# Batch 1's last three stores between batch 3's loads, one of them as five transfers, and batch 2's gather and MLP sooner

## The chip, the cores and the metric

The kernel runs on one core of one Trainium2 chip. The metric is the device time of one execution in microseconds, as a median over runs. The kernel before has a median of 256.77 us over 3 runs (256.72 to 257.05).

## The reference

Two stages over `q`, `k`, `v` of 4 batches x 6208 rows x 256 columns, all in f32:

```python
qn = q / (norm(q, axis=1) + 1e-06);  kn = k / (norm(k, axis=1) + 1e-06)   # over the rows
a = softmax(kn.transpose(0, 2, 1) @ qn / tau)       # 256 x 256 per batch
x = v @ a
scores[b] = x[b] @ w_gate                           # one number per row
top_idx = the 128 rows of the batch with the largest score
ye = relu(x[b, top_idx] @ w1) @ w2                  # w1 256x1024, w2 1024x256
out[b] = x[b];  out[b, top_idx] += sigmoid(scores[b, top_idx])[:, None] * ye
```

So every batch reads q, k and v once (6.36 MB each), writes its output once, and rewrites 128 rows of it.

## The kernel before

The rows of a batch are cut into chunks of 1024 rows, each as 128 partitions x 8 rows x 256 columns, and one remainder of 64 rows; `lorder` takes them as 0, remainder, 1, 2, 3, 4, 5. A load of a chunk reads 1 MB of f32 and writes 512 KB of bf16; all loads are issued by GpSimd (POOL) on its own queue (`emit_load`, L256). `pump` (L292) issues the next load when its buffer is free and the loads in flight are worth less than `AHEAD` = 12 us. Stores of a chunk are 128 partitions of 8 KB, 1 MB, issued by SyncE (SP) in `emit_store` (L721), called from `out_store` (L1098); batch 3's chunks go as two half stores.

A batch goes through these steps. TensorE multiplies q and k as they come (L448 and L452; for batch 3 L463, with norms apart); ScalarE and VectorE make the softmax from the sums (`softmax_stages`, L468). v is transposed on TensorE (`p2_transpose`, L572, matmul L583) and copied out of PSUM (L611, L614). The scores are products of the transposed v with `a @ w_gate` (L641, L651). `select_stages` (L737) then finds the 128 best rows: seven rounds of a comparison (L791), a counting matmul (L811) and a reduction (L815), then the index (L873), a gather of these 128 rows of v by POOL (L879), their transposes (L904), x of these rows (L919), the MLP (L945, ReLU L951, L967) and the update `upd` (L981), which POOL scatters into the output (L994) once the batch's stores have landed. Beside this, `p2_out` (L667) makes the output groups of 4 rows per partition: matmul L689, copy to a staging tile L707 or L704. There are 9 staging tiles.

What differs between the batches. All stores of batches 2 and 3 and those of batch 1's last two chunks are held until a gate, the landing of the first half of the last v load (`GATE`, L238, and the loop at L1142); one of batch 1's two is issued by POOL behind the last load. Batch 2's MLP is split: after its gather and first transposes the generator yields `("dead", f)` (L935 and L936), and goes on only when TensorE has ended batch 3's q/k products and their sums are read (`acc_dead`). Its last step, for batch 2, is a product by the gate on VectorE (L973) and three operations on POOL (L976 to L978). Batch 2's last two chunks (`LATE`) get their update as an added matmul (L696) and are stored last, from reused q/k tiles.

All engines' orders come from one loop (L1115) that models the engines and DMA rings and emits the instruction that is ready first, by priority. So a changed rule at one place moves other instructions too. Where TensorE would wait, the loop may put in fillers, matmuls whose result nobody reads (`unread`, L626, matmul L628); `PAUSE` = 0.05 us (L1079) is the shortest wait to which one is put.

## Time and profile before

| | |
|---|---|
| median of 3 runs | 256.77 us |
| the profiled execution | 256.67 us |
| its span | 254.9 us |
| TensorE's granted clock, mean | 0.989 |
| PE busy | 213.6 us (84%) |
| DVE busy | 105.1 us (41%) |
| ACT busy | 97.0 us (38%) |
| POOL busy | 58.8 us (23%) |
| DMA: loads' queue, share of 16 engines | 77.2% |
| DMA: stores' queue, share of 16 engines | 25.5% |

The span runs from the first to the last record of the profiled execution; the 1.77 us between it and the execution's own time lie around it. The engines' busy times are shares of the span, averages over stages with different limits. The two DMA queues run on the same 16 engines, and their shares together are over 100% because packets overlap.

### The profile page before, as it was taken

How to read it: one execution, taken by the hardware profiler on the slowest of the kernel's cores; microseconds unless marked ns; L12 is line 12 of the kernel's file. 1: busy time of each engine (PE TensorE's matmuls, PEld its weight loads, DVE VectorE, ACT ScalarE, POOL GpSimd, SP SyncE). 2: the span in 40 equal slices, each digit the busy share in tenths (PEclk: the TensorE clock that was granted, in tenths of full speed). 3: DMA queues.
4: the chain of work that ended last, by engine and by line, in shares of the span. 5: the costliest groups of instructions: out<-in, count | busy, mean ns of one | idle time of the engine just before them, and what ended most of it. 6: DMA issues, size and time to landing. Idle time of an engine off the chain costs nothing.

```text
span 254.9 us, 5961 instructions
## 1 busy us (share of the span) xinstructions
PE 213.6 (84%) x2516; PEld 169.0 (66%) x2516; DVE 105.1 (41%) x416; ACT 97.0 (38%) x181; POOL 58.8 (23%) x112
## 2 busy tenths in 40 slices
PE   0089877598998978999999896788999999999981
PEld 0068766445787864767678684677787788866870
DVE  0200001723774065431386400548767264777331
ACT  2800002730000278452435530571102289386650
POOL 8223122222302430120030232223212410030501
PEclk9999999999999999999999998999999999999998
DMA  6999999999999999999999999999999999999995
GB/s 235 261 217 211 214 215 212 214 211 214 213 214 213 211 231 287 286 311 319 296 316 282 325 301 211 213 212 214 212 213 211 212 212 265 418 422 419 389 416 235
DMA packets 16267, 66.82 MB, mean 262 GB/s; under 512 B 2097, under 2 KB 2866, under 8 KB 13042
## 3 DMA queue, kind: packets, MB, share of 16 engines
q0 software_dynamic: 12096, 39.98, 77.2%
q1 hardware_dynamic: 4146, 26.48, 25.5%
q8 instruction: 19, 0.31, 0.4%
q14 instruction: 6, 0.05, 0.0%
HBM read 78.91 MB, written 25.95 MB: 411 GB/s over the span
## 4 chain that ended last, share of the span: by engine, by line
PE 48%; DMA 32%; ACT 8%; DVE 7%; issue 2%; POOL 1%; POOLq 1%; DVEq 0%; ACTq 0%
DMA qk_ch<-in_k_dram 27%; PE s_ps L448 9%; PE g_ps L452 9%; PE o_ps L689 7%; DMA v_ch<-in_v_dram 5%; PE sc_ps L641 5%; PE vt_ps L583 4%; ACT vt_sb L611 4%; PE sc_ps L651 2%; PE m_ps L811 2%; PE o_ps L967 2%; DVE vt_sb L614 1%; ACT stage L707 1%; PE o_ps L945 1%; PE g_ps L689 1%
## 5 line engine op out<-in xcount | busy, mean ns | idle before, releaser
L448 PE MATMUL s_ps<-qk_ch 128*128 128x256 bf16 x288 | 67.5, 281 | 19.0 <-DMA qk_ch<-in_k_dram 19.0
L452 PE MATMUL g_ps<-qk_ch 128*128 128x256 bf16 x288 | 67.4, 281 | 0.0
L707 ACT COPY stage<-o_ps 128x512 f32<-128x512 f32 x71 | 40.3, 593 | 48.1 <-PE o_ps L689 47.3
L448 PEld LDWEIGHTS <-qk_ch 128*128 128x128 bf16 x288 | 29.0, 101 | 25.1 <-DMA qk_ch<-in_k_dram 20.1
L689 PE MATMUL o_ps<-a_sb,vt_sb 128*128 128x256 bf16 (+1 forms) x266 | 38.0, 272 | 2.3 <-ACT stage L707 1.4
L689 PEld LDWEIGHTS <-vt_sb 128*128 128x128 bf16 (+1 forms) x294 | 26.9, 97 | 9.5 <-issue 6.1
L452 PEld LDWEIGHTS <-qk_ch 128*128 128x128 bf16 x288 | 29.0, 101 | 4.4
L583 PEld LDWEIGHTS <-v_ch 128*128 128x128 bf16 x384 | 23.4, 98 | 7.7 <-issue 6.3
L583 PE MATMUL vt_ps<-ident_b,v_ch 128*128 128x128 bf16 x328 | 23.7, 219 | 3.6 <-ACT vt_sb L611 3.6
L488 DVE SCALAR_TENSOR_TENSOR junk<-g_ps,ident_f 128x128 f32<-128x128 f32 x6 | 1.7, 291 | 60.0 <-ACT e L479 59.9
L274 POOL DMA_DIRECT2D qk_ch<-in_q_dram x25 | 13.8, 551 | 47.9 <-DMA v_ch<-in_v_dram 15.5
L614 DVE COPY vt_sb<-vt_ps 128x1024 bf16<-128x1024 bf16 x21 | 14.3, 689 | 21.1 <-PE vt_ps L583 21.1
L274 POOL DMA_DIRECT2D v_ch<-in_v_dram x25 | 13.6, 551 | 26.1 <-DMA qk_ch<-in_q_dram 14.3
L274 POOL DMA_DIRECT2D qk_ch<-in_k_dram x25 | 13.5, 541 | 22.9 <-DMA v_ch<-in_v_dram 13.7
L791 DVE SCALAR_TENSOR_TENSOR cmp<-sc,wl,tab 128x392 bf16<-128x392 f32 x28 | 18.0, 643 | 1.0
L815 DVE TENSOR_REDUCE cnt<-m_ps 128x8 f32<-128x392 f32 (+2 forms) x28 | 12.0, 429 | 12.9 <-PE m_ps L811 12.9
L611 ACT COPY vt_sb<-vt_ps 128x1024 bf16<-128x1024 bf16 (+1 forms) x18 | 15.3, 900 | 1.1 <-PE vt_ps L583 1.1
L479 ACT COPY e<-g_ps 128x256 f32<-128x256 f32 x3 | 1.1, 372 | 38.2 <-PE g_ps L452 38.2
L641 PE MATMUL sc_ps<-vt_sb,awz 128*32 128x512 bf16 (+1 forms) x52 | 13.4, 368 | 0.6 <-DVE vt_sb L614 0.3
L879 POOL DMA_INDIRECT vg<-in_v_dram,idx x4 | 4.0, 1008 | 37.4 <-DVE idx L873 20.5
L463 PE MATMUL s_ps<-qk_ch 128*128 128x256 bf16 x96 | 12.0, 273 | 0.0
L994 POOL DMA_INDIRECT out_dram<-upd,idx x4 | 4.0, 996 | 29.6 <-DVE gej L820 19.6
(198 smaller groups left out, 291.9 us busy)
## 6 DMA issues: line engine op xcount, KB each, us to landing
out_dram<-stage SPq DMA_DIRECT2D x15, 1024.0 KB, 10.6
qk_ch<-in_q_dram POOLq DMA_DIRECT2D x23, 512.0 KB, 16.3
qk_ch<-in_k_dram POOLq DMA_DIRECT2D x23, 512.0 KB, 17.1
v_ch<-in_v_dram POOLq DMA_DIRECT2D x23, 512.0 KB, 15.1
out_dram<-stage SPq DMA_DIRECT2D x12, 512.0 KB, 6.2
stage<-in_moe_w_dram SPq DMA_DIRECT2D x2, 1024.0 KB, 5.0
out_dram<-qk_ch SPq DMA_DIRECT2D x2, 1024.0 KB
out_dram<-stage POOLq DMA_DIRECT2D x1, 1024.0 KB, 16.0
```

The source lines that it names most:

```text
L274: ins = nc.gpsimd.dma_start(out=t[:, rows, :], in_=lview(src, b, d)[:, rows, :])
L448: nc.tensor.matmul(s_ps[:, cc, :].rearrange("p (i c) -> p i c", i=2), lhsT=pair[:parts, 1, s, cc * P:(cc + 1) * P], rhs=pair[:parts, :, s, ...
L452: nc.tensor.matmul(g_ps[:, cc, :].rearrange("p (i c) -> p i c", i=2), lhsT=blocks[:parts, at, :], rhs=blocks[:parts, at:at + step + 1:step ...
L463: nc.tensor.matmul(s_ps[:, cc, :], lhsT=kt[:parts, s, cc * P:(cc + 1) * P], rhs=qt[:parts, s, :], start=d == FIRST and s == 0 and cc == 0, ...
L583: nc.tensor.transpose(vt_ps[:, cc, j, :], in_=vt[:, v0 + j, cc * P:(cc + 1) * P], identity=ident_b)
L611: nc.scalar.copy(to, frm)
L614: nc.vector.tensor_copy(to, frm)
L641: nc.tensor.matmul(t[0:2 * SG, 0:n * parts], lhsT=awz[:, cc, SX - m:SX - m + 2 * SG], rhs=vt_sb[:, cc, 0:n, :parts].rearrange("p j t -> p ...
L689: nc.tensor.matmul(o_ps[:parts, pj, :], lhsT=vt_sb[:, cc, j, :parts], rhs=a_sb[:, cc, :], start=pj == 0 and cc == 0, stop=last and cc == 1 ...
L707: nc.scalar.copy(st[:parts, rows, :], o_ps[:parts, :m, :])
L791: nc.vector.scalar_tensor_tensor(out=cmp, in0=sc[:, :, None].to_broadcast([P, NCOL, NTHR]), scalar=wl[:, i, NTHR:NTHR + 1], in1=tab[:, Non ...
L815: nc.vector.tensor_reduce(out=cnt9[:, 0:NTHR], in_=mps[:, 0:wide * NTHR].rearrange("p (s j) -> p j s", s=wide), axis=AX.X, op=ALU.add)
```

## The change

Five edits. (1) The stores of batch 1's chunks 1, 2 and 3 (`PACED`) are held in a list until `PACE`, the k load of batch 3's chunk 2, has been issued, and the stores wait for its landing. (2) The first of the three goes as five transfers of 64, 32, 25, 5 and 2 partitions: `SHARES` gives start, step and count, the steps being 2, 4, 4, 4 and 4. (3) `pump` looks only 6 us ahead between the point where batch 2's `a @ w_gate` is ready and batch 2's gather. (4) The `("dead", f)` yield is gone, so batch 2's MLP runs when its gather has landed; batch 2's output groups from the fifth on wait until batch 3's q/k products are all emitted. (5) `PAUSE` goes from 0.05 to 0.20 us.

```diff
@@ -205,6 +205,8 @@
     BACK = order[-2:]
+    PACED = [ci for ci in order if ci not in BACK][-3:]
+    SHARES = ((0, 2, 64), (1, 4, 32), (3, 4, 25), (103, 4, 5), (123, 4, 2))
     SG = 16
@@ -239,6 +241,7 @@
         GATE = ("v", 8) + units[-1]
+    PACE = ("k", 0) + ("qk", L, lorder[3])
     loaded = {}
@@ -289,12 +292,16 @@
 
+    aw_ready = {}
+    gathered = set()
+
     def pump():
         rings.run(now())
         flying[:] = [key for key in flying if rings.done.get(key, FAR) > now()]
         while nxt_unit[0] < len(units):
             u = units[nxt_unit[0]]
-            if not slots[bucket(u)] or sum(length[key] for key in flying) >= AHEAD:
+            ahead = 6.0 if E in aw_ready and E not in gathered else AHEAD
+            if not slots[bucket(u)] or sum(length[key] for key in flying) >= ahead:
                 return
@@ -368,7 +375,6 @@
     a_ready = {}
-    aw_ready = {}
     sc_tiles = {}
@@ -386,12 +392,12 @@
     deferred = []
+    paced = []
     gate_done = []
     late_inst = []
     late_add = []
     scatter_inst = {}
     store_inst = {b: [] for b in range(B)}
-    gathered = set()
     softmaxes = [0]
@@ -720,6 +726,16 @@
         st = stage_of[(b, ci)]
+        if (b, ci) == (E - 1, PACED[0]):
+            assert sum(n for _, _, n in SHARES) == P
+            made = []
+            for at, step, n in SHARES:
+                rows = slice(at, at + step * (n - 1) + 1, step)
+                made.append(nc.sync.dma_start(out=view(out, b, ci)[rows], in_=st[rows]))
+            sync_inst.extend(made)
+            transfers.extend(made)
+            store_inst[b].extend(made)
+            return made[0]
         if ci < NFULL:
@@ -932,8 +948,6 @@
         yield ("t", f)
-        if b == E:
-            yield ("dead", f)
         h_sb = moe.tile([P, NFC, P], BF16, name="h_sb")
@@ -1076,7 +1090,7 @@
     FILL = 0.4
-    PAUSE = 0.05
+    PAUSE = 0.20
     MARGIN = 0.3
@@ -1097,6 +1111,8 @@
         dep = stage_done[(b, ci)]
+        if b == E - 1 and ci in PACED:
+            dep = max(dep, rings.landing(PACE))
         if back(b, ci) and not gate_done:
@@ -1149,6 +1165,8 @@
                         reason="stores behind the last loads")
+        while paced and PACE in load_inst:
+            landed(out_store(*paced.pop(0)), load_inst[PACE], "stores between the last batch's loads")
         while late_ready and out_at == len(outs) and E in scatter_inst:
@@ -1183,6 +1201,8 @@
                 if b == 0 and sum(u[1] == 1 for u, _ in queue["p1"]) > HOLD:
+                    r = FAR
+                if b == E and queue["p1"] and gs.index(g) >= 4:
                     r = FAR
@@ -1266,6 +1286,8 @@
                     late_ready.append((b, g[0]))
+                elif b == E - 1 and g[0] in PACED:
+                    paced.append((b, g[0]))
                 elif b < E and back(b, g[0]) or back(b, g[0]) and not gate_done:
```

SP before, from batch 0's second store to the first half stores (`stage_rem` is a remainder's store); of the four whole stores behind the first remainder shown, three are batch 1's chunks 1, 2 and 3 and the fourth waits for the gate:

```order
L724 DMA out_dram<-stage 128x2048 x6
L726 DMA out_dram<-stage_rem 64x256
L724 DMA out_dram<-stage 128x2048 x4
L726 DMA out_dram<-stage_rem 64x256
L724 DMA out_dram<-stage 128x2048 x4
L724 DMA out_dram<-stage 64x2048 x2
```

and in the changed kernel:

```order
L740 DMA out_dram<-stage 128x2048 x6
L742 DMA out_dram<-stage_rem 64x256
L734 DMA out_dram<-stage 64x2048
L734 DMA out_dram<-stage 32x2048
L734 DMA out_dram<-stage 25x2048
L734 DMA out_dram<-stage 5x2048
L734 DMA out_dram<-stage 2x2048
L740 DMA out_dram<-stage 128x2048 x3
L742 DMA out_dram<-stage_rem 64x256
L740 DMA out_dram<-stage 128x2048 x4
L740 DMA out_dram<-stage 64x2048 x2
```

Chunk 1's store is five transfers now, and chunks 2 and 3 stand with the gated store; the rest keeps its order.

POOL before, in batch 3's last q and k loads and the v loads (`vg` is batch 2's gather), with the semaphores that each waits for:

```order
L274 DMA qk_ch<-in_q_dram 128x2048 [waits DMASW4_49,PE_49]
L274 DMA qk_ch<-in_k_dram 128x2048 [waits DMASW5_49]
L274 DMA qk_ch<-in_q_dram 128x1024 [waits DMASW6_49,PE_49]
L274 DMA qk_ch<-in_k_dram 128x1024 [waits DMASW7_49]
L274 DMA qk_ch<-in_q_dram 128x1024 [waits DMASW0_49]
L274 DMA qk_ch<-in_k_dram 128x1024 [waits DMASW1_49]
L274 DMA v_ch<-in_v_dram 128x2048 [waits DMASW2_49]
L879 DMA vg<-in_v_dram,idx 128x256 [waits DMASW3_49,DVE_49]
L276 DMA rem_in<-in_v_dram 16x1024 [waits DMASW4_49]
L274 DMA v_ch<-in_v_dram 128x2048 [waits DMASW5_49]
```

and now:

```order
L277 DMA qk_ch<-in_q_dram 128x2048 [waits DMASW4_49,PE_49]
L277 DMA qk_ch<-in_k_dram 128x2048 [waits DMASW5_49]
L895 DMA vg<-in_v_dram,idx 128x256 [waits DMASW6_49,DVE_49]
L277 DMA qk_ch<-in_q_dram 128x1024 [waits DMASW7_49,PE_49]
L277 DMA qk_ch<-in_k_dram 128x1024 [waits DMASW0_49]
L277 DMA qk_ch<-in_q_dram 128x1024 [waits DMASW1_49]
L277 DMA qk_ch<-in_k_dram 128x1024 [waits DMASW2_49]
L277 DMA v_ch<-in_v_dram 128x2048 [waits DMASW3_49]
L279 DMA rem_in<-in_v_dram 16x1024 [waits DMASW4_49]
L277 DMA v_ch<-in_v_dram 128x2048 [waits DMASW5_49]
```

The gather has moved ahead of the four half loads of q and k and of the first v load behind them.

POOL before, at the end of the loads (L724 is batch 1's store behind them; `upd` and `d_b` are batch 2's):

```order
L274 DMA v_ch<-in_v_dram 128x2048 x4
L274 DMA v_ch<-in_v_dram 128x1024 x2
L724 DMA out_dram<-stage 128x2048
L976 TENSOR_TENSOR upd<-e,xe 128x256
L977 CAST d_b<-e 128x256
L978 TENSOR_TENSOR d_b<-e,d_b 128x256
```

and now:

```order
L277 DMA v_ch<-in_v_dram 128x2048 x3
L990 TENSOR_TENSOR upd<-e,xe 128x256
L991 CAST d_b<-e 128x256
L992 TENSOR_TENSOR d_b<-e,d_b 128x256
L277 DMA v_ch<-in_v_dram 128x2048
L277 DMA v_ch<-in_v_dram 128x1024 x2
L740 DMA out_dram<-stage 128x2048
```

Batch 2's three operations stood behind all loads and a store; now three load issues and the store come after them.

## Rows read from the trace of the kernel before

**Rows 1.** The page's strips: DMA share in tenths and GB/s, 40 slices

```profile
DMA  6999999999999999999999999999999999999995
GB/s 235 261 217 211 214 215 212 214 211 214 213 214 213 211 231 287 286 311 319 296 316 282 325 301 211 213 212 214 212 213 211 212 212 265 418 422 419 389 416 235
```

**Rows 2.** The page's queues: kind, packets, MB, share of 16 engines

```profile
q8 instruction: 19, 0.31, 0.4%
```

**Rows 3.** Busy time by window, DMA share and GB/s last

```profile
core 0: us, PE busy (x) PEld busy (x) DVE busy (x) ACT busy (x) POOL busy (x), PEclk, DMA share, GB/s
180.00:200.00 20.00, 19.53 (x425) 15.63 (x423) 13.57 (x59) 3.22 (x7) 5.59 (x10) 1.00 1.08 212
200.00:212.00 12.00, 11.51 (x187) 9.90 (x185) 5.58 (x31) 7.07 (x15) 2.33 (x5) 1.00 1.07 212
217.00:225.00 8.00, 7.86 (x124) 6.66 (x121) 6.27 (x22) 4.33 (x9) 0.22 (x1) 1.00 1.00 416
232.00:239.00 7.00, 6.37 (x70) 5.17 (x71) 4.31 (x20) 3.88 (x8) 1.38 (x3) 1.00 1.01 420
239.00:241.00 2.00, 2.00 (x21) 1.79 (x19) 0.69 (x1) 1.28 (x3) 1.81 (x3) 1.00 0.93 338
```

**Rows 4.** DMA view of 250 to 254 us, columns of 0.1 us; then landing

```profile
DMA  9597795797792491191031059693012110000000
GB/s 410 246 655 328 328 655 246 328 655 328 328 655 82 164 573 82 82 410 82 0 164 82 0 246 492 246 451 123 0 82 82 82 41 0 41 0 0 0 0 0
...
out_dram<-upd,idx POOLq DMA_INDIRECT x1, 3.1
```

**Rows 5.** Chain of waits from 195 us on: start us, us, what

```profile
213.07 0.61 PE o_ps L945 x8
...
215.34 1.05 PE o_ps L967 x8
...
216.41 0.48 DVE e L973
...
244.26 1.31 PE sc_ps L628 x12
...
249.47 0.48 DVE upd L981
```

**Rows 6.** Timeline of POOL: start us, us, work, idle before and releaser

```profile
171.60 0.53 POOL L274 DMA_DIRECT2D qk_ch<-in_k_dram  x1 [1.69 <-DMA v_ch<-in_v_dram]
...
177.50 0.55 POOL L274 DMA_DIRECT2D qk_ch<-in_k_dram  x1
183.05 0.53 POOL L274 DMA_DIRECT2D qk_ch<-in_q_dram  x1 [5.00 <-PE m_ps L811]
...
189.15 0.53 POOL L274 DMA_DIRECT2D v_ch<-in_v_dram  x1 [1.98 <-DMA qk_ch<-in_q_dram]
196.12 0.99 POOL L879 DMA_INDIRECT vg<-in_v_dram,idx  x1 [6.44 <-DVE tokl L887]
...
204.20 0.53 POOL L274 DMA_DIRECT2D v_ch<-in_v_dram  x1 [1.97 <-DMA v_ch<-in_v_dram]
...
250.85 0.97 POOL L994 DMA_INDIRECT out_dram<-upd,idx  x1 [9.69 <-DMA out_dram<-qk_ch]
```

**Rows 7.** Timeline of SP, 130 to 160 us

```profile
133.67 8.89 SPq L724 DMA_DIRECT2D out_dram<-stage  x3
```

**Rows 8.** Waits of SP's queue: us in total, times, longest us

```profile
SPq L724 <- DMA v_ch<-in_v_dram: 73.0, 1, 73.0
```

**Rows 9.** The page's DMA issues: count, KB each, median us to landing

```profile
qk_ch<-in_k_dram POOLq DMA_DIRECT2D x23, 512.0 KB, 17.1
...
stage<-in_moe_w_dram SPq DMA_DIRECT2D x2, 1024.0 KB, 5.0
```

**Rows 10.** Timeline of PE, 218.6 to 221 us

```profile
219.02 0.61 PE L583 MATMUL vt_ps<-ident_b,v_ch 128*128 128x128 bf16 x8
```

## The prediction

> **What bounds the kernel now.** I read the page's strips first. The DMA strip stands at 9 (90% or more) in every slice but the first and the last, and the bytes fall into two levels, 211 to 215 GB/s where the casting loads run and about 420 GB/s where only stores run [rows 1]. The windows give the same without rounding: a share of 1.08 in 180 to 200 us and 1.07 in 200 to 212 at 212 GB/s, then 1.00 at 416 GB/s in 217 to 225 and 1.01 at 420 in 232 to 239 [rows 3]. So the transfers are the bound from the start to about 251 us; TensorE's granted clock is 1.00 (2.4 GHz, the upper level) in all these windows. The page's queue part says what else these engines carry: 19 instruction fetches that take 0.4% of 16 engines' span [rows 2], 0.004 x 16 x 254.9 / 19 = 0.86 us for one.
>
> Then the end, drawn in tenths of a microsecond [rows 4]. One packet of a store is a partition's 8 KB, so 82 GB/s in a tenth is one packet. Added up by three columns, the strip has 16, 16, 15 and 16 packets (one on each of 16 engines) up to 251.2 us, then 10, 7 and 3: six engines have run out of stores by 251.2, three more by 251.5, four more by 251.8, and about three go on alone. From column 23 on the last scatter (rows of 1 KB) passes on the engines that are free, 246 to 492 GB/s for half a microsecond, and what follows until 253.5, single eighties, is the three late engines. The scatter was issued at 250.85 us [rows 6] and landed 3.1 us later [rows 4], at 253.95; the span ends 0.95 us after. So the end is set by three late engines, although every store is spread evenly over all of them. 16 engines cannot share 19 fetches of 0.86 us evenly, which is the kind of thing that makes some late.
>
> The chain of waits has another account of the same end: MLP (L945, L967), upd at 249.47 + 0.48 = 249.95 us, the scatter behind it [rows 5]. Both are true within a microsecond: on the free engines the scatter's rows are through in columns 23 to 27, by 252.8 us, 0.7 before the late ones.
>
> **The change part by part.** The bytes are the same: loads and stores only stand in another order, and transfers that are full before and after end no sooner for that. In the windows a stretch of whole stores (217 to 225) and one of half stores (232 to 239) move at 416 and 420 GB/s [rows 3]; I take the reorder at 0. What the change can win is idle time of single engines: share 0.93 in 239 to 241 [rows 3], 0.07 x 2 x 16 = 2.2 us of one engine, and the lateness at the end.
>
> *The three stores of batch 1.* Before, SP issues them from 133.67 us on [rows 7] and then waits 73.0 us for the gate, the first half of the last v load [rows 8]. Now all three wait for k of batch 3's chunk 2. That load is issued at 171.60 us [rows 6] and a k load lands 17.1 us after issue [rows 9], so they start at about 188.7. SP issues nothing else in between; behind the new wait on its queue stand only the stores that wait for the gate anyway. The three tiles are held 50 us longer, so batch 2's output groups from the fifth on move behind batch 3's q/k products: TensorE's work in another place. Cost 0; where ScalarE's copies for want of a tile came late, they would delay the v stretch by a copy or two of 0.6 us, which the transfers cover.
>
> *The five transfers.* The store of 128 partitions becomes 64, 32, 25, 5 and 2. Four more issues: the price of an issue lies between nothing (half stores at 420 GB/s against 416 for whole ones) and 2.5 us each, from the weights' loads of 1,024 KB, which land 5.0 us after issue [rows 9] where 1.0486 MB at 424 GB/s takes 2.47; 4 x 2.5 = 10 us is the upper end. I take 0, since the half stores are the nearest row: twelve of them in the tail and no gap. The Trainium skill (DMA: Bandwidth & Descriptors, Anatomy of one DMA — SWDGE (gpsimd) path) gives each transfer about 2.0 us fixed cost; that would be 8 us here if it were paid in the engines' time, and the 420 GB/s of the half stores do not show it.
>
> What the split does is to load engines unequally. A row of 8 KB costs an engine 2.47 / 8 = 0.31 us, which is also the period of the strip in [rows 4]. 64 and 32 rows go 4 and 2 to an engine. 25, 5 and 2, together 32 rows, do not divide by 16; 25 and 5 divide by five. If they go to five engines, these have 6 + 32/5 = 12.4 rows (+4.4, +1.36 us) and eleven have 6 instead of 8: -2 rows, -0.62 us. By the bounds, an engine can lose between 0 and 2 rows (0 to -0.62) and the heaviest can gain up to 32 - 2 = 30 (+9.3, all on one engine); I take five engines. The Trainium skill (same page, Why a DMA increments its semaphore by 16 and not by 1) says that a transfer runs on the largest number of engines up to 16 that divides its partitions, on the lowest-numbered ones: 13 rows on two engines, 12 on three, 6 on eleven, which no run so far shows. What it does to the end depends on who the five are. Six engines lead the last three by 253.5 - 251.2 = 2.3 us [rows 4], more than 1.36; if the five are among those ahead, the late three win 0.62 us. The seven in between (through by 251.5 to 251.8) would then be at 252.9 to 253.2, about level with 253.5 - 0.62 = 252.9. No row names the engines. The Trainium skill (same page, Latency and other measured facts) calls engines 7 and 15 usually slower, on a cause that it only guesses; these would be among the eleven.
>
> *Batch 2's MLP sooner.* In batch 3's chain of waits stand L945 0.61, L967 1.05 and the DVE step 0.48, together 2.14 us around 213 to 217 [rows 5]; v's last transposes come at 219.02 us [rows 10], with stores already running at 416 GB/s. This work goes to where TensorE multiplies batch 3's q and k. Of the fillers, 12 in 1.31 us before the last MLP [rows 5], nine stand in the new order: 3 x 0.11 = 0.33. So upd comes up to 2.1 + 0.3 us sooner, between 0 and that. It is worth nothing beyond what the late engines leave: the scatter's rows queue behind the stores on these. But it keeps the chain clear of the earlier drain, so I count 0 and let it hold up the 0.62.
>
> *The gathers.* Batch 2's gather now stands ahead of four half loads and one of v, which POOL issued from 183.05 to 189.15 us. POOL stood 6.44 us for that gather's index, until 196.12 [rows 6], and the share stayed at 1.08 [rows 3]. If the index comes no sooner, POOL now stands from the end of the load before, 177.50 + 0.55 = 178.05, to 196.12: 18.1 us in which it issues no load. The cover: that last load lands at 177.50 + 17.1 = 194.6, and the three paced stores are 3 x 2.47 = 7.4 us more, to 202. So 0, with some 6 us of room less the time that the next load takes to start; without the stores in it the engines would stand from 194.6 to the gather's end at 197.1, 2.5 us, and this is the price of a failed cover; with that much room I give it no chance of its own. Batch 1's gather moves behind two more loads, the safe direction. Batch 2's three POOL operations, now between v loads, take the place of waits for a landing such as the 1.97 us at 204.20 [rows 6].
>
> The sum: span 254.9 - 0.62 = 254.28, plus 1.77 (256.67 of the profiled execution less its span) = 256.05 us. The median of the runs is 256.77, 0.10 above the profiled execution: 256.15. I say 256.1.
>
> **Rivals.** *No effect.* The rows fall on engines that include some of the late ones in part, or the fetches move to other engines with the new instruction order, and the late ones stay as late: 256.7. For it: only the last three engines count and 19 fetches can fall anew. Against it: an engine's share of that store does change. *The heavy rows on late engines.* One of the five is one of the last three: 4.4 x 0.31 = +1.36, and with 4 or 5 rows +1.24 or +1.55, so 257.9 to 258.3, about 258.1. It decides as soon as one engine that is less than 1.36 us ahead of the last gets them. For it: drawn by lot, five of 16 miss all three in 3 of 10 cases. Against it: an engine that is behind is so through its fetches, and the five that have fewest are as many as the leading group; I do not go by the lot. *The chain sets the end.* If upd's 2.1 us are what counts and the late engines catch up too: 256.7 - 2.1 = 254.6. For it: the chain runs through that MLP [rows 5]. Against it: three engines still drain stores when the scatter's other rows are through [rows 4]. *The price of a transfer is paid*, in full: 256.7 + 10 = 266.7; for it only the weights' loads [rows 9], against it the half stores.
>
> **The numbers.** The forecast has a chance of 0.62, its own range 255.6 to 256.5 (from a gain of 0.2, where the late three keep part of it, to 1.1, where half a fetch falls elsewhere too); no effect 0.19; heavy rows on late engines 0.12; the chain 0.05; the price 0.02. A measurement of this kernel tells about 0.2%, 0.51 us, from no change. The forecast is 0.11 us above that bound, so of its 0.62 I put 0.50 beyond it and 0.12 within. Faster is 0.50 + 0.05 = 0.55, same 0.12 + 0.19 = 0.31, slower 0.12 + 0.02 = 0.14. The range for 8 in 10 goes from 255.4 to 257.4: it holds the forecast and no effect and leaves out the heavy case (0.12), the chain (0.05) and the price (0.02).
>
> **What would show it.** In the changed profile the strip of the last four microseconds should keep 16 packets in a round to about 251 us and end at 252.9 instead of 253.5; five transfers stand in SP's row behind k of batch 3's chunk 2, with the share at 1.0 or above beside them; upd ends near 247.6 us; POOL's wait for batch 2's index leaves no dip. It is wrong if the last engines go on alone for over 2 us after the rest, if the DMA share dips while POOL waits, or if upd comes before 248 and the end with it.

## The result, and the profile after

The changed kernel takes 257.89 us (median of 13 runs, 257.14 to 260.25), the kernel before 256.75 (13 runs, 256.60 to 257.05): a ratio of 1.0055, 95% interval 1.0033 to 1.0077. (A ratio here weighs all runs of its set except those more than 1.5% above the fastest of their kernel, so it can differ from the ratio of two medians, which is 1.0044 here.) It is slower by 1.1 us where 0.6 us less was forecast, and above the range. Its runs also scatter over 3 us, those of before over half a microsecond. The profiled execution took 258.70 us, with a span of 256.7 and a granted clock of 0.978 (before 256.67, 254.9 and 0.989); it lies above the median, so the trace shows the loss larger than the median has it.

The page's strips of the changed kernel, 40 slices, answer to [rows 1]:

```profile
DMA  6999999999999999999999999999999999999995
GB/s 237 262 215 213 215 214 215 211 213 215 211 213 213 213 244 289 279 320 322 292 308 219 220 210 214 216 211 213 268 341 237 206 212 267 377 425 411 404 426 221
```

The share says 9 as before, so this strip alone hides the loss. Batch 1's stores have left the mixed stretch (slices 22 to 24 are at 210 to 220 GB/s now) and stand in slices 29 and 30. The windows show more; these columns answer to [rows 3]:

```profile
core 0: us, PE busy (x) PEld busy (x) DVE busy (x) ACT busy (x) POOL busy (x), PEclk, DMA share, GB/s
...
184.00:192.00 8.00, 7.90 (x178) 6.28 (x177) 5.57 (x27) 0.79 (x2) 0.61 (x1) 1.00 1.03 324
192.00:200.00 8.00, 7.88 (x121) 6.17 (x120) 2.55 (x14) 2.02 (x4) 5.31 (x10) 1.00 1.05 244
194.00:195.00 1.00, 0.88 (x18) 0.58 (x18) 0.53 (x3) 0.58 (x3) 1.00 (x3) 1.00 0.83 261
200.00:208.00 8.00, 7.67 (x134) 6.01 (x133) 3.87 (x22) 2.85 (x6) 3.55 (x7) 1.00 1.07 208
...
220.00:224.00 4.00, 3.93 (x42) 3.32 (x40) 2.67 (x11) 3.25 (x7) 0.00 (x0) 1.00 0.89 363
```

Beside the paced stores the bytes rise to 324 GB/s. In the single microsecond from 194 the share is 0.83. From 200 to 208 us, loads alone again, 208 GB/s move at a share of 1.07, and in 220 to 224 the share is 0.89 where all should be stores at full rate. The two queues of 192 to 200 us (packets, MB, share):

```profile
q0 software_dynamic: 627, 0.97, 74.9%
q1 hardware_dynamic: 139, 0.95, 28.7%
```

A load's written byte costs twice a stored one: loads alone move 212 GB/s [rows 1, 3], stores alone 416 to 425 ([rows 3] and the strip above); a load reads 1 MB for the 512 KB that it writes. So I count the work in a window as the loads' MB over 0.2125 MB/us and the stores' over 0.425: 0.97 / 0.2125 = 4.56 us and 0.95 / 0.425 = 2.24, together 6.80 us of work in 8 us. The kernel before has only loads in these eight:

```profile
q0 software_dynamic: 727, 1.66, 108.7%
```

By the same measure that is 1.66 / 0.2125 = 7.81 us. The changed kernel loses 1.0 us here. What POOL does there answers to [rows 6]:

```profile
170.03 0.55 POOL L277 DMA_DIRECT2D qk_ch<-in_k_dram  x1
191.39 0.99 POOL L895 DMA_INDIRECT vg<-in_v_dram,idx  x1 [20.81 <-DVE tokl L903]
192.37 0.59 POOL L277 DMA_DIRECT2D qk_ch<-in_q_dram  x1
192.89 0.67 POOL L277 DMA_DIRECT2D qk_ch<-in_k_dram  x1
...
204.37 0.72 POOL L990 TENSOR_TENSOR upd<-e,xe 128x256 f32<-128x256 f32 x1 [4.39 <-DVE e L987]
...
250.69 0.97 POOL L1008 DMA_INDIRECT out_dram<-upd,idx  x1 [10.02 <-DVE seen_sb L1006]
```

After the load at 170.03 POOL issues nothing for 20.81 us, until batch 2's index lets the gather go at 191.39; the next loads follow half a microsecond apart. The gather is earlier than in the kernel before (196.12), but the load ahead of it is earlier too, 170.03 against 177.50, since batch 1's three stores, 7.4 us of transfers, no longer run before (in a run without paced stores, below, it is issued at 177.41 again). On SP the five transfers and the other two stores follow from 178.74 us on, ten microseconds sooner than I had put them:

```profile
178.74 3.47 SPq L734 DMA_DIRECT2D out_dram<-stage  x5
```

SP's first store behind the gate, in the kernel before and in the changed one:

```profile
215.57 0.33 SPq L724 DMA_DIRECT2D out_dram<-stage  x1
217.74 0.33 SPq L740 DMA_DIRECT2D out_dram<-stage  x1
```

It goes out 2.17 us later, and the execution is 2.03 us longer (258.70 against 256.67). So the loss of this trace is there when the last loads land, before the last stores begin.

And the tail, 252 to 256 us in columns of 0.1 us, answers to [rows 4]:

```profile
DMA  9959959955997642412310420300100000000000
GB/s 492 573 246 492 573 246 410 655 246 246 492 369 328 246 164 123 164 82 82 164 82 0 205 82 41 123 0 41 41 41 0 0 0 0 0 0 0 0 0 0
```

Sixteen packets in a round of three columns stand up to 252.9; the tail of a few engines then goes on to 255, about 2.1 us, where it was 2.3 (251.2 to 253.5). That is one of the signs that the prediction had named for being wrong. The last MLP's update, meanwhile, has not moved as forecast:

```profile
202.60 1.10 PE o_ps L981 x8
...
249.04 0.49 DVE upd L995
```

Batch 2's MLP runs at 202.60 (1.10 us for L981, the former L967), off its old place, but `upd` of batch 3 ends at 249.53, against 249.95 before [rows 5] and 247.6 forecast.

### The profile page after: what moved, and what is told of

Read it like the earlier page. It is cut to its first block, busy times and chain, and to the rows that moved or that the text cites. A ratio compares the mean times of both kernels' runs of the same rounds, so it can differ in the third digit from the quotient of the medians.

```text
span 256.7 us, 5993 instructions
## 1 busy us (share of the span) xinstructions
PE 215.7 (84%) x2529; PEld 171.4 (67%) x2529; DVE 105.9 (41%) x417; ACT 96.2 (37%) x180; POOL 58.7 (23%) x112
## 4 chain that ended last, share of the span: by engine, by line
PE 59%; DMA 18%; ACT 12%; DVE 6%; issue 2%; POOLq 1%; POOL 0%; ACTq 0%; DVEq 0%
DMA qk_ch<-in_k_dram 12%; PE s_ps L454 11%; PE g_ps L458 11%; PE o_ps L695 9%; PE vt_ps L589 6%; PE sc_ps L647 5%; PE s_ps L469 4%; ACT stage L713 4%; DMA out_dram<-stage 3%; DMA vg<-in_v_dram,idx 3%; ACT vt_sb L617 3%; PE g_ps L439 3%; PE sc_ps L657 2%; PE m_ps L827 2%; ACT e L550 1%
## 5 line engine op out<-in xcount | busy, mean ns | idle before, releaser
L454 PE MATMUL s_ps<-qk_ch 128*128 128x256 bf16 x288 | 65.9, 277 | 16.6 <-DMA qk_ch<-in_k_dram 16.6
L458 PE MATMUL g_ps<-qk_ch 128*128 128x256 bf16 x288 | 65.9, 277 | 0.0
L713 ACT COPY stage<-o_ps 128x512 f32<-128x512 f32 x73 | 41.5, 595 | 44.7 <-PE o_ps L695 44.2
L454 PEld LDWEIGHTS <-qk_ch 128*128 128x128 bf16 x288 | 28.5, 99 | 22.0 <-DMA qk_ch<-in_k_dram 17.4
L695 PE MATMUL o_ps<-a_sb,vt_sb 128*128 128x256 bf16 (+1 forms) x270 | 39.2, 275 | 2.9 <-ACT stage L713 1.9
L458 PEld LDWEIGHTS <-qk_ch 128*128 128x128 bf16 x288 | 28.6, 99 | 4.0
L589 PEld LDWEIGHTS <-v_ch 128*128 128x128 bf16 x384 | 25.0, 102 | 8.5 <-issue 6.7
L589 PE MATMUL vt_ps<-ident_b,v_ch 128*128 128x128 bf16 x336 | 26.8, 230 | 3.9 <-ACT vt_sb L617 3.9
L620 DVE COPY vt_sb<-vt_ps 128x1024 bf16<-128x1024 bf16 x22 | 15.0, 690 | 23.1 <-PE vt_ps L589 23.1
L807 DVE SCALAR_TENSOR_TENSOR cmp<-sc,wl,tab 128x392 bf16<-128x392 f32 x28 | 17.5, 626 | 1.0
L617 ACT COPY vt_sb<-vt_ps 128x1024 bf16<-128x1024 bf16 (+1 forms) x17 | 14.4, 895 | 0.5 <-PE vt_ps L589 0.5
L864 ACT CAST excl_b<-m_ps 128x50 bf16<-128x50 f32 x3 | 0.6, 201 | 32.5 <-PE m_ps L857 32.5
L469 PE MATMUL s_ps<-qk_ch 128*128 128x256 bf16 x96 | 12.2, 273 | 0.0
## 6 DMA issues: line engine op xcount, KB each, us to landing
qk_ch<-in_k_dram POOLq DMA_DIRECT2D x23, 512.0 KB, 17.8
```

The lines of the kernel that those rows point to most:

```text
L454: nc.tensor.matmul(s_ps[:, cc, :].rearrange("p (i c) -> p i c", i=2), lhsT=pair[:parts, 1, s, cc * P:(cc + 1) * P], rhs=pair[:parts, :, s, ...
L458: nc.tensor.matmul(g_ps[:, cc, :].rearrange("p (i c) -> p i c", i=2), lhsT=blocks[:parts, at, :], rhs=blocks[:parts, at:at + step + 1:step ...
L469: nc.tensor.matmul(s_ps[:, cc, :], lhsT=kt[:parts, s, cc * P:(cc + 1) * P], rhs=qt[:parts, s, :], start=d == FIRST and s == 0 and cc == 0, ...
L589: nc.tensor.transpose(vt_ps[:, cc, j, :], in_=vt[:, v0 + j, cc * P:(cc + 1) * P], identity=ident_b)
L617: nc.scalar.copy(to, frm)
L620: nc.vector.tensor_copy(to, frm)
```

## The experiments

The expectations name these theories: A, POOL stands before batch 2's gather with no load to issue and the loads run down; B, the uneven split makes engines late; C, stores among batch 3's loads cost in themselves; D, the held outputs leave too few finished stores when the loads are in; F, the softmax's wait through a shared tile; G, TensorE's idle time and lowered clock before batch 3's softmax. Ratios are to the kernel before in the same set of runs. Some edits build on others; each is named by what it adds.

**The split.** First, one transfer in place of five (the branch on `PACED[0]` removed):

```diff
-        if (b, ci) == (E - 1, PACED[0]):
...
-            return made[0]
```

> The changed kernel with chunk 1's store of batch 1 as one transfer of 128 partitions again, all else as changed. Theory A (batch 2's gather stands ahead of four half loads, POOL issues no load from 170.6 to 191.4 us, and the loads run down: 1.2 us of transfer time lost at 190 to 206 us): about 257.9, as the changed kernel, since the gather stays there. Theory B (the uneven split makes some engines later, by up to 4 or 5 rows of 0.31 us): 256.4 to 256.7. The prediction's own step (the split gives 0.62 us): 258.5.

257.40 us, ratio 1.0049 (1.0017 to 1.0081): not told apart from the changed kernel, and not the 0.6 us slower that the prediction's step asks for. Then the split alone, that branch and `SHARES` put into the kernel before:

> The kernel before with nothing but the five transfers for batch 1's chunk 1, at the store's old place behind 133 us. Theory A: 256.7, the split neither costs nor gives. Theory B: 257.5 to 258.3. The prediction's own step: 256.1.

256.89 us, ratio 1.0010 (1.0001 to 1.0019). At its old place the split gives no 0.62 us and costs at most 0.2%: the prediction's step falls, and B as the cause.

**Two edits that met another wait.** The look-ahead, and the yield put back:

```diff
-            ahead = 6.0 if E in aw_ready and E not in gathered else AHEAD
+            ahead = AHEAD
```

> The changed kernel with the look-ahead of the loads at 12 us throughout (the 6 us rule between batch 2's a @ w_gate and its gather left out): the gather of batch 2 then stands behind the four half loads of q and k, one place ahead of where it stood before; paced stores, the split and the missing yield stay. Theory A: 256.5 to 256.9, POOL without load to issue only for some 6 to 10 us, the transfers without a dip at 190 to 200 us. Theory B: 257.9, no difference. Theory C (the stores moved out of 130 to 150 us into batch 3's loads cost, wherever the gather stands): 257.9.

```diff
+        if b == E:
+            yield ("dead", f)
         h_sb = moe.tile([P, NFC, P], BF16, name="h_sb")
```

> The changed kernel with the wait of batch 2's MLP for the end of batch 3's q and k products put back; the gather stays ahead of the four half loads. Theory A: 257.9 or a little more (the MLP's 2 us return to the path between the last loads and the outputs, hidden by the stores). If the early MLP itself disturbs (its work on TensorE and ScalarE lets q/k buffers come free later): 256.8.

273.68 us (1.0662) and 274.67 (1.0710): all expectations missed, by 16 to 18 us. The waits of the first of them between 205 and 232 us (total, times, longest):

```profile
POOL upd L990 <- issue: 17.8, 1, 17.8
...
PE o_ps L695 <- ACT stage L713: 17.0, 1, 17.0
DVE e L548 <- POOL d_b L992: 16.8, 1, 16.8
```

Batch 2's product by the gate stands in the softmax's tile `e`. Where the MLP comes too late, POOL's three operations stand behind the drain that follows POOL's last store, 17.8 us; VectorE's L548 of batch 3's softmax waits for the last of them, L992, and all of batch 3 behind it. So these two say nothing on A; they show a price of the early MLP that the diff doesn't.

**The drain behind the three operations.** `late_add` holds batch 2's three operations on POOL once they are issued; with the drain's condition on it, the drain comes after them. Added to the look-ahead run, then with other parts taken away:

```diff
-        if nxt_unit[0] == len(units) and not drained and E in gathered and len(behind) == BEHIND:
+        if nxt_unit[0] == len(units) and not drained and late_add and len(behind) == BEHIND:
```

> The changed kernel with the look-ahead at 12 us throughout, and POOL's drain after the last store put behind batch 2's three POOL operations (in the trace of the look-ahead run they stood behind it, 17.7 us, and batch 3's softmax waited for the tile they read). Batch 2's gather stands behind the four half loads; paced stores, split and early MLP stay. Theory A (loads run down while POOL stands before the gather): 256.5 to 256.9, and no stall at 210 to 230 us. Theory C (stores among batch 3's loads cost in themselves): 257.5 to 257.9.

260.10 us, 1.0138 (1.0097 to 1.0179), above both expectations: the softmax still waits for the same tile, now 2.0 us (L548 for L992).

With one store for the five as well (the first experiment's edit):

> As the first of these runs, with chunk 1's store as one transfer. Theory A: the same 256.5 to 256.9. Theory B (the uneven split makes engines later): faster than the first of these runs by 0.3 to 0.6 us.

258.77 us, 1.0065 (1.0050 to 1.0081), again a miss for A, with the same wait of 2.0 us. It is 1.3 us faster than with five transfers and the two intervals do not meet, which is B's way and more than B's amount; the runs of the two sets lie between 257.5 and 262.1 us, and no other pair shows it. So a cost of the split in this order is not excluded. Without paced stores and with the gather early:

```diff
-            ahead = 6.0 if E in aw_ready and E not in gathered else AHEAD
+            ahead = 3.0 if E in aw_ready and E not in gathered else AHEAD
...
-                elif b == E - 1 and g[0] in PACED:
-                    paced.append((b, g[0]))
```

> Batch 1's three stores at their old place, whole, and batch 2's gather still ahead of the four half loads (look-ahead 3 us in that stretch), early MLP, drain behind the three POOL operations. Theory A: nothing covers POOL's wait now. The last loads before it land near 188 us, the next ones are issued at about 192 us: 4 to 6 us without transfers, 260.5 to 262.5. Theory C: 256.7, since the stores are back.

261.12 us, 1.0173 (1.0160 to 1.0186), inside A's numbers and far from C's; the softmax does not wait for POOL here (its wait, 2.9 us, is for ScalarE). POOL's timeline and the strip of 188 to 200 us (0.3 us a column) of that run:

```profile
177.41 0.55 POOL L277 DMA_DIRECT2D qk_ch<-in_k_dram  x1
194.88 1.00 POOL L885 DMA_INDIRECT vg<-in_v_dram,idx  x1 [16.92 <-DVE tokl L893]
```

```profile
DMA  9999999999999999997656633000289757969999
GB/s 205 219 219 218 218 205 219 259 205 191 191 218 218 218 205 218 205 191 150 123 109 123 150 68 68 0 0 0 14 94 147 53 82 109 143 109 143 164 157 178
```

The share runs down from 193.4 us on, and three columns, 195.5 to 196.4, are empty; before and after them only some engines work. So the paced stores do cover a part of POOL's stand, worth 3.2 to 4.0 us (261.12 less the 257.89 and 257.12 of two sets of runs with the paced stores, whose index came earlier, at 191.39 and 190.50). The same with the gather behind the half loads (`ahead = 6.0`):

> As the run before with look-ahead 6 us, by which the gather stands behind the four half loads: only the early MLP, the pause of the fillers and the drain's place are left of the change. Theory A: 256.5 to 256.9. If the early MLP costs by itself: 257.5 and more.

258.94 us, 1.0082 (1.0061 to 1.0103): a miss for A alone, with the tile's wait in it as in the two above.

**Another buffer.** Batch 2's product in a buffer of the MLP, so that the softmax waits for nobody; the drain's condition is as above, and the look-ahead 12.0:

```diff
-            d_f = smx.tile([P, 2, D], F32, name="e")[:, 0, :]
+            d_f = moe.tile([P, 2, D], F32, name="h_sb")[:, 0, :]
```

> As the look-ahead run with the drain moved, and batch 2's product by the gate is put into a buffer of the MLP (h_sb) instead of the tile that batch 3's softmax needs next. Gather of batch 2 behind the four half loads; pace, split, early MLP, held outputs stay. Theory A (what the changed kernel loses is the run-down of the loads before the gather, 1.2 us): 256.5 to 256.9. Theory C (stores among batch 3's loads cost in themselves): 257.5 to 257.9. Theory D (the held outputs leave too few finished stores when the last loads are in): 257.2 and more, with the transfers' share below 0.7 at 221 to 226 us.

257.31 us, 1.0025 (1.0008 to 1.0042). POOL's gather, then windows of this run (258.04 us):

```profile
191.60 1.00 POOL L895 DMA_INDIRECT vg<-in_v_dram,idx  x1 [9.36 <-DVE tokl L903]
```

```profile
212.00:214.00 2.00, 0.95 (x15) 0.72 (x12) 1.67 (x8) 2.00 (x4) 0.00 (x0) 1.00 1.05 222
216.00:218.00 2.00, 2.00 (x21) 2.00 (x20) 1.38 (x2) 0.04 (x1) 0.00 (x0) 0.50 0.89 361
222.00:224.00 2.00, 1.93 (x17) 1.50 (x16) 1.32 (x7) 1.64 (x4) 0.00 (x0) 1.00 0.66 277
```

```profile
q0 software_dynamic: 579, 1.06, 70.8%
q1 hardware_dynamic: 164, 1.16, 36.3%
```

POOL waits 9.36 us only, and the loads do not run down (by the two queues of 192 to 200 us, shown last, 7.72 us of work). But TensorE, busy for 0.95 of 2 us at 212, has a granted clock of 0.50 (1.2 GHz) at 216, the outputs come late, and the transfers' share falls to 0.66 at 222. A is not the whole, and what D expected, 257.2 and more with a share below 0.7, is what came.

> The changed kernel with that other buffer and the drain's place, gather ahead of the four half loads as changed. Theory A: 257.5 to 258.2, as the changed kernel, since the run-down stays. If the shared tile itself held up the changed kernel: 256.9.

257.15 us, 1.0023 (1.0009 to 1.0038), with the look-ahead of 6.0 back and so the gather ahead as in the changed kernel: between the two expectations. Then the same without the `paced` list and the split, by which the gather falls behind the half loads:

> No paced stores and no split, gather of batch 2 behind the four half loads, early MLP in its own buffer, outputs held. Theory A: 256.5 to 256.9. Theory D: 257.2 and more.

257.06 us, 1.0026 (1.0009 to 1.0044): above A's numbers and below D's. It is 4.1 us less than the 261.12 us of the earlier set with the gather ahead and no paced stores, so without that cover the gather's place costs some 4 us (the look-ahead, which sets the place, and the buffer of batch 2's product are what differs between these two). Its profiled run, 256.91 us, shows neither a lowered clock at 212 to 224 us nor a share below 0.98 at 216 to 226; where the slower runs of this set, up to 259.31, lose their time was not seen.

Then, with the look-ahead 12.0 again, the held outputs let go too:

```diff
-                if b == E and queue["p1"] and gs.index(g) >= 4:
-                    r = FAR
```

> No paced stores, no split, look-ahead 12 us (the gather at its old place), outputs not held: the kernel before but for the missing yield, the MLP's own buffer, the drain's place and the pause of 0.20 us. Theories A and D: 256.4 to 256.8. If the early MLP costs by itself: 257.5.

256.84 us, 1.0001 (0.9993 to 1.0010), within 0.3 us from run to run. With the gather at its old place, no pace and no held outputs, the kernel before is back; in that order the missing yield and the longer pause of the fillers cost nothing. (By the code `PAUSE` is the time from one filler to the next; the shortest wait that is filled is `FILL`, 0.4 us.) There the gather lands so late that the MLP runs at its old place too, so an early MLP was not tested by this. Nor were the held outputs (D) tested alone.

**Is it the tile or the clock?** Four runs: the drain's condition alone (every engine's order is then the changed kernel's, so this is a second trace of it); six more fillers; one store; the fillers again. The last two have the own buffer and its drain.

> The changed kernel with only the condition of the drain changed; every engine's order is that of the changed kernel, so this is also a second trace of it. If the shared tile is what the own-buffer run took away: 257.5 to 258.3 with single runs at 259 and more, as the changed kernel. If the drain's place did it: 257.15.

257.12 us, 1.0023 (1.0012 to 1.0034). The same instructions gave 1.0055 (1.0033 to 1.0077) in the first set: how many of a set's runs come out a microsecond or more above the rest differs from set to set, and what the own buffer seemed to win (1.0023) was this. F falls.

```diff
-                unread()
+                for _ in range(10 if acc_dead[0] and L not in a_ready else 1):
+                    unread()
```

> The changed kernel with six more fillers where TensorE waits for ScalarE's copy before batch 3's softmax is out, at 212.5 to 214 us (0.66 us of matmuls whose result nobody reads). Theory G (the early MLP leaves TensorE idle there, 0.9 of 2 us in 212 to 214, its granted clock drops to 0.50 in some runs, the outputs come late and the stores run dry): the runs at 258.7 to 260.3 are gone, median 257.2 to 257.5. Theory F (the wait of the softmax for POOL's operations, the shared tile): no change, 257.9 with the same high runs.

257.38 us, 1.0040 (1.0017 to 1.0064), with a run at 259.53.

> The own-buffer kernel with the gather ahead of the half loads (257.15), chunk 1's store as one transfer. The prediction's step: 257.6 to 257.8, 0.62 slower. The split costs (13 rows on some engines): 256.8 to 257.0. The split does nothing: 257.15.

257.17 us, 1.0016 (1.0007 to 1.0025); its profiled run, 259.31 us, is the highest of its twelve. Against 1.0023 for the own buffer with the split, nothing either way.

> The own-buffer kernel with the six fillers. Theory G: the one run at 259.3 of twelve does not come again, median 256.9 to 257.1, the clock 1.00 in 212 to 222 us. Theory F alone: 257.15 as before.

257.45 us, 1.0048 (1.0027 to 1.0068), with a run at 261.01: the fillers change nothing in the times. They fill about half of the gap (TensorE is busy for 1.49 of 2 us in 212 to 214, for 0.85 in the second trace), and the clock is 1.00 there in both, so G is not excluded by them. But the first trace, 258.70 us, has its loss with a clock of 1.00 from 208 to 224 us, so G is not needed for a long run.

**The index.** The traces with the gather ahead and paced stores differ in when the index comes. The gather and the queues of 192 to 200 us in the second trace (257.13 us) and in the own-buffer run with one store (259.31 us):

```profile
190.50 1.00 POOL L895 DMA_INDIRECT vg<-in_v_dram,idx  x1 [20.00 <-DVE tokl L903]
```

```profile
q0 software_dynamic: 695, 1.12, 79.2%
q1 hardware_dynamic: 135, 0.93, 28.2%
```

```profile
192.79 0.99 POOL L885 DMA_INDIRECT vg<-in_v_dram,idx  x1 [22.24 <-DVE tokl L893]
```

```profile
q0 software_dynamic: 533, 0.82, 65.8%
q1 hardware_dynamic: 158, 1.07, 32.5%
```

Work in the eight microseconds: 1.12 / 0.2125 + 0.93 / 0.425 = 7.46 us, and 0.82 / 0.2125 + 1.07 / 0.425 = 6.38. With the changed kernel's trace the gather at 190.50, 191.39 and 192.79 goes with 7.46, 6.80 and 6.38 us of work and with 257.13, 258.70 and 259.31 us. The other four such traces fall in line: 190.55, 190.59, 190.85 and 191.16 us with 7.41, 7.46, 7.04 and 7.11 us of work and 257.10, 257.35, 257.50 and 257.49 us. SP's first store behind the gate follows: 216.18 us in the second trace, 217.74 in the first, 218.05 in the one of 259.31.

Between the two traces of the same instructions the index's delay, 0.89 us, is already there at the first comparison of batch 2's seven rounds (L807), at 175.21 us in the first and 174.32 in the second. Before that stands a stretch at the lower clock, first trace first:

```profile
164.00:170.00 6.00, 6.00 (x94) 5.75 (x92) 2.76 (x4) 1.54 (x4) 1.81 (x4) 0.50 1.06 210
164.00:170.00 6.00, 6.00 (x109) 5.56 (x107) 3.11 (x5) 1.69 (x4) 2.03 (x5) 0.72 1.06 210
```

TensorE, busy for 0.80 us of the two before 163 in both, has a granted clock of 0.50 (1.2 GHz) throughout these six microseconds in the first and for part of them in the second. My reading is that batch 2's rounds come later by that. The kernel before has such a stretch too (0.87 and 0.70 in 154 to 158 and 158 to 162 us). Why it is longer in the first trace is open, and in the other late traces it is no longer than in the second, so their delay has another source. To move the index on purpose, five more operations of 0.30 us on VectorE ahead of it, in both kernels:

```diff
+        if b == E:
+            for _ in range(5):
+                nc.vector.tensor_scalar_mul(dmx, ident_f, mx)
         idx = moe.tile([P, 1], I32, name="idx", bufs=3)
```

> The changed kernel with five idle VectorE operations of 0.30 us (the product that makes dmx, again) ahead of batch 2's index: the index comes 1.5 us later, every engine's order else as it was. Theory A (POOL stands before the gather with no load issued, so what the index loses the loads lose): the median 1.3 to 2 us above the changed kernel's, 258.5 to 259.5, and the work moved in 192 to 200 us below 6.8. If the run-down is covered by the paced stores: 257.1 to 257.9, no difference.

258.25 us, 1.0067 (1.0054 to 1.0079), between the two expectations: only 0.4 us above the first set's median, with intervals that meet (1.0055, 1.0033 to 1.0077), but clear of the second set (1.0023, 1.0012 to 1.0034). All its runs lie from 258.00 to 259.15, where the lowest of the two sets are 257.14 and 256.95. Its trace (258.33 us):

```profile
169.97 0.55 POOL L277 DMA_DIRECT2D qk_ch<-in_k_dram  x1
191.90 1.00 POOL L898 DMA_INDIRECT vg<-in_v_dram,idx  x1 [21.38 <-DVE tokl L906]
```

```profile
q0 software_dynamic: 596, 0.91, 70.7%
q1 hardware_dynamic: 135, 0.93, 28.4%
```

0.91 / 0.2125 + 0.93 / 0.425 = 6.47 us of work, 1.0 less than in the second trace, and the execution is 1.2 us longer than that one's. The two make a matched pair: the first of the seven rounds (174.36 and 174.32 us) and an operation just ahead of the five added ones (L885, 189.56 and 189.51) come within 0.05 us of each other. Then the gather is 1.40 us later, and so is, by 1.03 us, the first store behind the gate (second trace, then this one):

```profile
216.18 0.33 SPq L740 DMA_DIRECT2D out_dram<-stage  x1
217.21 0.33 SPq L740 DMA_DIRECT2D out_dram<-stage  x1
```

The delay does not go by the MLP: batch 2's POOL operations and the last v loads stand 0.3 us earlier in it than in the second trace (203.53 and 205.28 against 203.84 and 205.60). Its granted clock is 0.56 and 0.58 in 216 to 218 and 218 to 220 us, where the transfers' share stays at 0.96 or more, and 1.03 of its 1.2 us are lost by then, so the clock makes little of its loss.

> The kernel before with the same five operations ahead of batch 2's index. Theory A: 256.6 to 256.9, no difference, since the gather stands behind all q and k loads and the first v load there, and 1.5 us more of POOL's wait (6.44) are covered by loads issued before it. If a later index costs wherever the gather stands: 257.5 to 258.3.

256.65 us, 0.9999 (0.9991 to 1.0008). In its trace the index comes 1.2 us later, 197.34 against 196.12 [rows 6], and the loads do not notice:

```profile
189.11 0.53 POOL L274 DMA_DIRECT2D v_ch<-in_v_dram  x1 [1.95 <-DMA qk_ch<-in_q_dram]
197.34 1.00 POOL L882 DMA_INDIRECT vg<-in_v_dram,idx  x1 [7.70 <-DVE tokl L890]
```

```profile
q0 software_dynamic: 724, 1.64, 107.9%
```

1.64 / 0.2125 = 7.72 us of work, as before (7.81). A later index costs where the gather stands ahead of the half loads, about its own delay, and nothing where it stands behind them. So A is shown as a cause, by the dose and by the place; how much of the loss is A's is another question, taken up at the end of the next section.

## Why the prediction was wrong

*What bounds the kernel.* Right: the transfers bound it, and where they fall behind the end moves with them.

*The five transfers, -0.62 us.* This step failed. I took the lateness at the end for something that a one-time shift of load before it would relieve. The split alone gives 1.0010, and with one store in place of five 1.0049 and, with the own buffer, 1.0016 stand beside 1.0055 and 1.0023 with five; a fourth pair, on the look-ahead run, has the split slower. In the changed kernel the tail of a few engines is still 2.1 us long. My reading, which no view can show since none names an engine, is that who is late is settled again after 180 us by what each engine still gets. That instruction fetches make the late ones late was not tested either. I had also no row that named the engines, and gave 0.62 to it nevertheless.

*The gathers, 0.* This is the step that failed where the time was lost: the wait was taken as covered and put at nothing. I had the place (POOL from the last load to the index, 18.1 us; measured 20.81) and the cover (the loads in flight and three stores, to 202 us), and priced a failed cover at 2.5 us, "with that much room" at no chance. Two things were wrong in it. The start: with the stores taken out of the stretch before, the loads run 7.4 us ahead, so the last load goes out at 170.03 and not at 177.50, and the index, though 5 us sooner, does not make that up. With 170.03 the same sum, 170.03 + 17.1 + 7.4, ends the cover at 194.5 us, 3.1 us after the gather's issue instead of 6, and from 194 to 195 the share is 0.83, just behind POOL's wait. And the cover was counted as one sum for 16 engines, while the shares point to engines that run dry one after another: in single microseconds from 191 to 195 the share only falls to 0.95 and 0.83, yet 0.35 us of work are lost in a good run (7.46 against 7.81) and 1.0 to 1.4 in a bad one. It was not given back: the four traces with 0.35, 1.0, 1.3 and 1.4 us lost are 0.5, 2.0, 1.7 and 2.6 us longer than that of the kernel before (256.67).

*Batch 2's MLP sooner, 0.* Right that nothing is won, though `upd` did not come 2 us sooner but 0.4. Not seen: the product stands in the tile of batch 3's softmax, a wait on POOL's queue, harmless in the changed order (POOL is done at 206.2 us, the softmax asks at 210.4) and worth about 17 us in two nearby ones.

*The rivals.* The first set's median fits the rival of the heavy rows (257.9 to 258.3), but its mechanism does not: the split alone costs 0.2% at most. The price of a transfer paid in full, 10 us, was excluded by the split alone: four more transfers cost 0.08 us in the median. The Trainium skill (DMA: Bandwidth & Descriptors, Anatomy of one DMA — SWDGE (gpsimd) path) gives a transfer on GpSimd's path about 2.0 us of fixed cost and lays it mostly to completion; these stores are SP's, and 4 x 2.0 us is not seen in the engines' time here.

*Still open.* How much of the loss is A's. In the second trace 0.35 of 0.5 us are lost in 192 to 200; in the first 1.0 of 2.0 are lost there, and by the gate the whole 2 us are lost before the last stores begin, so the share of 0.89 at 220 to 224, where finished outputs are missing, is not needed for it. But with the gather behind the half loads and an own buffer the kernel is no faster (1.0025 with paced stores, 1.0026 without): taking A away does not bring the time back. One trace with paced stores shows another way to lose it, an idle TensorE before the softmax, a clock of 0.50 and stores that run dry; for the runs without paced stores no trace shows the loss. The held outputs (D) stand in both and were only taken out together with other edits. A lowered clock at 216 to 220 us stands in two more of the longer traces (0.56 with the late index, 0.50 in the one of 259.31 us), not in the first. The sets of runs were not all taken on the same chip, and the chip's part in their scatter was not tested. No version beat the kernel before.

## What to carry to other kernels

A gather on the queue that issues the loads is a gate: put it behind as many loads as the wait for its index is long, and count that wait from the last issue in the new order, not in the old trace. Cover for such a gap should be counted as what the first engine to run dry still has, not as the sum of what is in flight. And before a fine correction of the engines' balance is worth a term of its own, look at whether anything between it and the end deals the load out again.

## What was not expected of the hardware

No fixed price of a transfer showed: SP issued five of 64, 32, 25, 5 and 2 rows within 3.47 us, and the split alone cost 0.08 us. The same instructions scattered by 0.3% between two sets of runs, 1.0055 and 1.0023, while the medians of the kernel before stayed within 0.2 us of 256.7 in all of them. In the two traces of these instructions the index differs by 0.89 us, behind a stretch at the lower clock some 20 us ahead of it that is longer in the one than in the other, and the delay went on to the loads and to the end; in the kernel before an index 1.2 us later changed nothing.
